# Earlier first evacuations, one tile loaded ahead of the weights, moved mask copies, and the last block projected by seven products, in a fused attention and SwiGLU kernel

## The chip, the cores and the metric

The kernel runs on one core of a Trainium2 chip. The time is device time of one execution in microseconds (us), the median of several runs. The profile is that of one execution; its span is some 1.7 to 2.1 us shorter than the time of the same run.

Engines: TensorE (PE) multiplies, VectorE (DVE) and ScalarE (ACT) read PSUM, compute and write SBUF, GpSimd (POOL) and SyncE (SP) mostly issue transfers here.

## The reference

Sliding-window attention with a distance bias, then a gated feed-forward layer:

```python
# q, k, v: (8, 8, 576, 64)   window 128
scores = np.where(mask, scale * (q @ k.T) + bias, -1e9)
attn = softmax(scores) @ v                   # (8, 8, 576, 64)
x = attn.transpose(0, 2, 1, 3).reshape(4608, 512)
g, val = x @ w_gate, x @ w_val               # (4608, 1536)
return (g * sigmoid(g) * val) @ w_out        # (4608, 512)
```

## The kernel before

Attention goes by units of 128 queries, 36 in all. The feed-forward layer goes by nine blocks of 512 tokens. For each block, 12 gate products (`pg`) and 12 value products (`pv`), each four matmuls of 512 columns, give the hidden rows `hT`. After a gate product ScalarE takes tanh (`tt`) and VectorE makes `uu` = (tanh + 1) times gate, and `hT` is `uu` times the value product. A projection (`po`) with `w_out` follows. Other names in the traces: `pt` are transposes of k and q (`kn`, `qn`), `ps` and `psc` scores, `ex` and `exc` their exponentials, `av` the product with v, `x` the attention output, `px` its transposes, `osb` output rows in SBUF on their way to a store.

In the traces here TensorE works through its instructions in the order in which they were built.

```python
        for i in range(FIRST):              # the first four units, a tile (128 tokens) each
            ...
            if i >= 2:
                begin(4, i - 1)             # gate and value products m=0, 1 over the tiles that exist
            if i > 0:
                x_transposed(i - 1)
        begin(6, 2)
        begin(4, 3)
        x_transposed(FIRST - 1)
        begin(6, 3)
        # cut: evacuation starts only with the full 512 columns, in gate_val

    load_qk(5, "k"); load_v(5)              # written on one line here
    load_w(1024, 1536)                      # last slices of w_gate and w_val, 512 KB each
    load(6)                                 # k, q, v of tile 6
```

Blocks 1 to 7 are projected by Strassen's scheme: the block as 2x2 quarters, seven products of 6 matmuls for each half in place of eight. The last block was not; it had 12 matmuls of 512 columns for each of three row groups and 24 of 256 for the fourth:

```python
        for j in range(3):
            for _ in project(NBLK - 1, j, ps_a, "a", 4):
                yield 1.0
        yield from last_project(NBLK - 1, 3)     # two halves of 256 columns, each stored by itself
```

The softmax here doesn't subtract the row's maximum and nothing guards it: scores larger than these inputs give would overflow.

## Time and profile before

| | before |
|---|---|
| time, median of 3 runs | 357.24 us (357.01 to 357.49) |
| span of the profiled run | 355.1 us |
| TensorE busy | 341.5 us (96%) |
| first scores of all (`ps`) start | 8.90 us |
| scores of unit 6 start | 44.81 us |
| first projection of block 0 (`po`) starts | 54.62 us |
| last block's projection, start to end | 340.65 to 351.20 us |
| behind it, to the end of the span | 3.9 us |

The prediction shows the lines on the ramp and the tail's products. The order of time on TensorE (start, duration, engine, line, operation, operands, shape, count) where the scores of unit 6 stand, and where the first projection of block 0 follows:

```profile
44.50 0.38 PE L368 MATMUL pg<-xT,wg_sb 128*128 128x512 f16 x1
44.81 0.62 PE L254 MATMUL ps<-qT,kT 64*128 64x256 f16 x8
...
54.62 1.24 PE L398 MATMUL po<-wo_sb,hT 128*128 128x512 f16 x5
```

The row to remember is the one at 44.81: exactly 9.81 us lie between it and the first `po`.

The DMA view of the last 17 us (345 to 362), in 40 slices of 0.425 us: busy tenths, GB/s, and issues with the number, the size and the median time to landing.

```profile
DMA  3994005895003997805800000000000000000000
GB/s 82 207 227 101 0 0 120 173 222 121 0 0 77 207 231 164 236 10 113 195 0 0 0 0 0 0 0 0 0 0 0 0 0 0 0 0 0 0 0 0
...
out_dram<-osb SPq DMA_DIRECT2D x5, 128.0 KB, 2.4
out_dram<-osb ACTq DMA_DIRECT2D x2, 64.0 KB, 2.2
out_dram<-osb SPq DMA_DIRECT2D x2, 64.0 KB, 2.1
```

The output leaves in bursts with pauses (the zeros) between them: each row group is stored while the next is projected. Only the last two half stores stand at the end.

### The profile page before, as it was taken

The numbers are of one execution on the slowest core, as the hardware profiler recorded it, in microseconds if no ns is written. First come the engines' busy times: TensorE is split into PE (matmuls) and PEld (weight loads), VectorE is DVE, ScalarE is ACT, GpSimd is POOL, SyncE is SP. The second block draws the span as 40 slices with busy tenths as digits, with TensorE's granted clock in tenths as the row PEclk, the third lists the DMA queues.
The fourth block names the chain that finished last, engine by engine and source line by source line (L and its number), as shares of the span: only waits on it lengthen the run. The fifth ranks groups of instructions, "written<-read, shape, count | busy, mean of one in ns | idle before, by whom it ended". The sixth has DMA issues, their size and how long they took to land.

```text
span 355.1 us, 7251 instructions
## 1 busy us (share of the span) xinstructions
PE 341.5 (96%) x2765; PEld 196.8 (55%) x2765; DVE 273.1 (77%) x595; ACT 178.2 (50%) x353; POOL 106.9 (30%) x132
## 2 busy tenths in 40 slices
PE   7898999999999999999999999999999999999995
PEld 4683454544456655565456655564666566456643
DVE  4858786997977799678986998799878965975540
ACT  4847584555555454555555555455444323332321
POOL 8964755544838354543500100000000000000000
PEclk9999999999999999999999999999999999999999
DMA  9999999999999999999995413311022101101114
GB/s 150 171 186 188 136 184 153 92 149 129 154 134 178 155 147 170 169 144 166 181 73 105 66 55 30 90 31 59 17 75 55 50 2 59 62 0 62 39 43 96
DMA packets 157763, 37.34 MB, mean 105 GB/s; under 512 B 147232, under 2 KB 153248, under 8 KB 157728
## 3 DMA queue, kind: packets, MB, share of 16 engines
q0 software_dynamic: 116224, 18.62, 84.3%
q1 hardware_dynamic: 41056, 17.97, 27.5%
q8 instruction: 21, 0.34, 0.4%
q10 hardware_dynamic: 448, 0.30, 0.3%
q14 instruction: 14, 0.11, 0.1%
HBM read 37.91 MB, written 9.44 MB: 133 GB/s over the span
## 4 chain that ended last, share of the span: by engine, by line
PE 71%; DVE 11%; DMA 6%; ACT 5%; POOL 4%; issue 3%; DVEq 0%; ACTq 0%; POOLq 0%
PE pg L368 21%; PE pv L368 21%; PE po L477 14%; PE av L319 4%; DMA qn<-in_q_dram 4%; PE po L398 3%; PE ps L254 3%; DVE uu L381 2%; DVE hT L385 2%; PE p L477 2%; DMA wv_sb<-in_moe_w_val_dram 2%; ACT ex L259 2%; PE px L345 2%; DVE ex L263 2%; ACT exc L286 1%
## 5 line engine op out<-in xcount | busy, mean ns | idle before, releaser
L368 PE MATMUL pg<-xT,wg_sb 128*128 128x512 f16 (+2 forms) x464 | 116.4, 365 | 0.3 <-ACT xT L346 0.2
L368 PE MATMUL pv<-xT,wv_sb 128*128 128x512 f16 (+2 forms) x464 | 114.7, 365 | 1.6 <-DVE uu L381 1.6
L379 ACT ACTIVATE tt<-pg 128x512 f16<-128x512 f32 x108 | 65.1, 604 | 85.7 <-PE pg L368 82.3
L381 DVE SCALAR_TENSOR_TENSOR uu<-tt,pg 128x512 f16<-128x512 f16 x107 | 73.0, 683 | 38.1 <-ACT tt L379 37.7
L385 DVE TENSOR_TENSOR hT<-uu,pv 128x512 f16<-128x512 f16 x108 | 73.7, 682 | 6.1 <-PE pv L368 2.3
L368 PEld LDWEIGHTS <-wv_sb 128*128 128x128 f16 x464 | 42.7, 98 | 38.8 <-issue 3.1
L368 PEld LDWEIGHTS <-wg_sb 128*128 128x128 f16 x464 | 42.4, 98 | 35.1 <-issue 2.9
L259 ACT ACTIVATE ex<-ps 128x512 f16<-128x512 f32 x96 | 50.1, 605 | 9.8 <-PE ps L254 9.8
L168 POOL DMA_DIRECT2D va<-in_v_dram x40 | 34.1, 856 | 50.3 <-PE av L319 36.0
L174 POOL DMA_DIRECT2D qn<-in_q_dram x39 | 33.6, 864 | 27.9 <-DMA qT<-qn 19.6
L174 POOL DMA_DIRECT2D kn<-in_k_dram x39 | 33.2, 860 | 25.6 <-DMA kT<-kn 15.7
L477 PEld LDWEIGHTS <-hT 128*128 128x128 f16 x336 | 31.8, 98 | 15.4 <-issue 3.5
L263 DVE TENSOR_TENSOR ex<-ex,m_reg 128x1024 f16<-128x1024 f16 x48 | 32.5, 686 | 8.3 <-ACT ex L259 8.3
L477 PEld LDWEIGHTS <-S 128*128 128x128 f16 x252 | 23.9, 98 | 11.7 <-issue 2.9
L322 DVE TENSOR_TENSOR x<-av,rec 128x256 f16<-128x256 f32 x72 | 28.9, 419 | 0.6
L477 PE MATMUL po<-T,S 128*128 128x256 f16 x168 | 23.0, 273 | 0.6 <-ACT p5s L495 0.6
L477 PE MATMUL po<-T,hT 128*128 128x256 f16 x168 | 23.1, 272 | 0.4
L286 ACT ACTIVATE exc<-psc 128x512 f16<-128x512 f32 x40 | 21.4, 608 | 3.4 <-PE psc L282 3.4
L346 ACT COPY xT<-px 128x512 f16<-128x512 f16 x24 | 14.1, 586 | 15.3 <-PE px L345 15.3
L319 PEld LDWEIGHTS <-ex 128*128 128x128 f16 x384 | 18.4, 97 | 4.9 <-issue 0.7
L319 PE MATMUL av<-va,ex 128*128 128x65 f16 x384 | 20.4, 193 | 0.5
L398 PE MATMUL po<-wo_sb,hT 128*128 128x512 f16 x84 | 19.7, 379 | 0.0
(74 smaller groups left out, 289.7 us busy)
## 6 DMA issues: line engine op xcount, KB each, us to landing
out_dram<-osb SPq DMA_DIRECT2D x32, 256.0 KB, 2.5
va<-in_v_dram POOLq DMA_DIRECT2D x32, 128.0 KB, 8.6
qn<-in_q_dram POOLq DMA_DIRECT2D x31, 128.0 KB, 8.7
kn<-in_k_dram POOLq DMA_DIRECT2D x31, 128.0 KB, 8.1
wo_sb<-in_moe_w_out_dram POOLq DMA_DIRECT2D x2, 768.0 KB, 9.4
wg_sb<-in_moe_w_gate_dram POOLq DMA_DIRECT2D x2, 512.0 KB, 10.7
wv_sb<-in_moe_w_val_dram POOLq DMA_DIRECT2D x2, 512.0 KB, 11.8
out_dram<-osb SPq DMA_DIRECT2D x6, 128.0 KB, 2.4
```

The source lines that it names most:

```text
L168: nc.gpsimd.dma_start(va[rank][p0:p1, :, 0:D], src)
L174: nc.gpsimd.dma_start(t_[p0:p1], src)
L259: nc.scalar.activation(e[:, o:o + 2, :], banks[q4][par], AF.Exp, scale=scale)
L263: nc.vector.tensor_mul(e[:, o, :], e[:, o, :], reg[:, o, :])
L319: nc.tensor.matmul(av[:, j, :], w, val, start=(n == 0), stop=(n == len(todo) - 1))
L322: nc.vector.tensor_mul(x[:, 4 * half:4 * half + 4, :], av[:, :, 0:D], rec.broadcast_to([P, 4, D]))
L368: nc.tensor.matmul(ps[:, c0:c1], w[:, kb, ms], xT[n][:, kb, c0:c1], start=(kb == 0 and c0 == 0), stop=(kb == NKB - 1 and c1 == 512))
L379: nc.scalar.activation(tt, pg, AF.Tanh, scale=0.5)
L381: nc.vector.scalar_tensor_tensor(out=uu, in0=tt, scalar=one if (n, m) == PIN else 1.0, in1=pg, op0=ALU.add, op1=ALU.mult)
L385: nc.vector.tensor_mul(hT[n][:, m, :], uu, pv)
L398: nc.tensor.matmul(po, hT[n][:, m, j * P:(j + 1) * P], wo_sb[:, m, :], start=(i == 0), stop=(i == NMB - 1))
L477: nc.tensor.matmul(dst, a[:, m, cols], b[:, m, :], start=(start and m == 0), stop=(m == HM - 1), skip_group_check=True)
```

## The change

It is meant to shorten both ends. On the ramp, the first two gate and value products are evacuated for the 384 tokens that exist, ahead of the last 128; k and q of tile 6 are loaded ahead of the last weight slices, as TensorE waits for that q; the mask copies leave the crowded stretch. At the end, the last block gets the seven products. The core of the diff:

```diff
+MASKS_AT = 18.0
@@ first_tiles
         begin(6, 2)
         begin(4, 3)
+        gate(0, 0, early[(0, 0, "g")][0], 0, 384)
         x_transposed(FIRST - 1)
+        val(0, 0, early[(0, 0, "v")][0], 0, 384)
+        gate(0, 1, early[(0, 1, "g")][0], 0, 384)
+        val(0, 1, early[(0, 1, "v")][0], 0, 384)
         begin(6, 3)
@@ loads
     load_qk(5, "k")
+    load_qk(6)
     load_v(5)
     load_w(1024, 1536)
-    load(6)
+    load_v(6)
@@ everything
-                if at == 5.0:
-                    make_masks()
         for step in steps:
+            if step == MASKS_AT:
+                make_masks()
@@ ffn, the last block
-        for j in range(3):
-            for _ in project(NBLK - 1, j, ps_a, "a", 4):
-                yield 1.0
-        yield from last_project(NBLK - 1, 3)
+        ends = [strassen(NBLK - 1, t) for t in range(2)]
+        for t in 7 * (0, 1):
+            next(ends[t])
+            yield 0.75
@@ strassen (end: the last block; t: its half)
+        if end and t:
+            store(n, t + 2, low, HC, DM, True)
...
-        nc.scalar.mul(low[:, 0:HC], X, 0.5)
-        (stores of top and low, all on SyncE)
+        store(n, t, top, 0, DM, end)             # end: the second of the two on ScalarE's queue
...
+        if end and t:
+            nc.vector.tensor_scalar_mul(low[:, 0:HC], X, 0.5)
+        else:
+            nc.scalar.mul(low[:, 0:HC], X, 0.5)
+        store(n, t + 2, low, 0, HC if end and t else DM, end)
```

Cut from it: the split of `gate_val` into `gate` and `val` over a range of columns, PSUM and SBUF buffers for the second half's copies, and the sums of `hT` for the last block.

More of the change, by code (lines that the diff above doesn't have):

```diff
@@ L368, in wide @@
             nc.tensor.matmul(ps[:, c0:c1], w[:, kb, ms], xT[n][:, kb, c0:c1],
-                             start=(kb == 0 and c0 == 0), stop=(kb == NKB - 1 and c1 == 512))
+                             start=(kb == 0 and c0 == 0), stop=(kb == NKB - 1 and c1 == 512),
+                             skip_group_check=(n == 0))
         if c1 < 512:
@@ L372, in wide, with gate, val, gate_val @@
         return ps
-    def gate_val(n, m):
+    acted = {}
+    def gate(n, m, pg, c0=0, c1=512):
+        if (n, m) not in acted:
+            acted[(n, m)] = [supool.tile([P, 512], FP16, name=i, tag=i) for i in ("tt", "uu")]
+        tt, uu = (t_[:, c0:c1] for t_ in acted[(n, m)])
+        nc.scalar.activation(tt, pg[:, c0:c1], AF.Tanh, scale=0.5)
+        nc.vector.scalar_tensor_tensor(out=uu, in0=tt, scalar=one if (n, m) == PIN else 1.0,
+                                       in1=pg[:, c0:c1], op0=ALU.add, op1=ALU.mult)
+    def val(n, m, pv, c0=0, c1=512):
         if n not in hT:
             hT[n] = hpool.tile([P, NMB, 512], FP16, name="hT", tag="hT")
-        pg = wide(n, m, "g")
-        tt = supool.tile([P, 512], FP16, name="tt", tag="tt")
-        nc.scalar.activation(tt, pg, AF.Tanh, scale=0.5)
-        uu = supool.tile([P, 512], FP16, name="uu", tag="uu")
-        nc.vector.scalar_tensor_tensor(out=uu, in0=tt, scalar=one if (n, m) == PIN else 1.0, in1=pg,
-                                       op0=ALU.add, op1=ALU.mult)
+        nc.vector.tensor_mul(hT[n][:, m, c0:c1], acted[(n, m)][1][:, c0:c1], pv[:, c0:c1])
+    def gate_val(n, m):
+        c0 = 384 if (n, m) in acted else 0
+        gate(n, m, wide(n, m, "g"), c0)
         yield
-        pv = wide(n, m, "v")
-        nc.vector.tensor_mul(hT[n][:, m, :], uu, pv)
+        val(n, m, wide(n, m, "v"), c0)
         yield
@@ L391, in rows_of, with store @@
         return [(0, 128, n * S + j * P)]
+    def store(n, j, osb, c0=0, c1=512, two=False):
+        for i, (p0, p1, r0) in enumerate(rows_of(n, j)):
+            (nc.scalar if two and i else nc.sync).dma_start(out[r0:r0 + p1 - p0, c0:c1],
+                                                            osb[p0:p1, c0:c1])
     def project(n, j, pool, tag, bufs):
@@ L402, in project @@
                 nc.scalar.mul(osb, po, 0.5)
-                for p0, p1, r0 in rows_of(n, j):
-                    nc.sync.dma_start(out[r0:r0 + p1 - p0, :], osb[p0:p1, :])
+                store(n, j, osb)
             yield
-    def last_project(n, j):
-        osb = opool.tile([P, DM], FP32, name="osb", tag="osb")
-        for half in range(2):
-            c = slice(half * DM // 2, (half + 1) * DM // 2)
-            po = ps_a.tile([P, DM // 2], FP32, name="po", tag="a", bufs=4)
-            for m in range(NMB):
-                nc.tensor.matmul(po, hT[n][:, m, j * P:(j + 1) * P], wo_sb[:, m, c],
-                                 start=(m == 0), stop=(m == NMB - 1))
-            if half == 0:
-                nc.scalar.mul(osb[:, c], po, 0.5)
-            else:
-                nc.vector.tensor_scalar_mul(osb[:, c], po, 0.5)
-            for i, (p0, p1, r0) in enumerate(rows_of(n, j)):
-                (nc.sync if i == 0 else nc.scalar).dma_start(out[r0:r0 + p1 - p0, c], osb[p0:p1, c])
-            yield 1.5
     HM = NMB // 2
@@ L467, in strassen @@
         cols = slice(t * P, (t + 1) * P)
-        po = ps_f.tile([P, 2, HC], FP32, name="po", tag="po", bufs=1)
+        end = n == NBLK - 1
+        pool, tag, bufs = (ps_a, "a", 4) if end and t else (ps_f, "po", 1)
+        po = pool.tile([P, 2, HC], FP32, name="po", tag=tag, bufs=bufs)
         p2 = ps_a.tile([P, HC], FP32, name="p2", tag="a")
         top, low = (opool.tile([P, DM], FP32, name="osb", tag="osb") for _ in range(2))
-        p1s = supool.tile([P, HC], FP32, name="p1s", tag="p1s", bufs=1)
-        p5s = supool.tile([P, HC], FP32, name="p5s", tag="p5s", bufs=1)
-        u2s = supool.tile([P, HC], FP32, name="u2s", tag="u2s", bufs=1)
+        if end and t:
+            spare = [opool.tile([P, DM], FP32, name="osb", tag="osb") for _ in range(2)]
+            p1s, p5s, u2s = spare[0][:, 0:HC], spare[0][:, HC:DM], spare[1][:, 0:HC]
+        else:
+            p1s, p5s, u2s = (supool.tile([P, HC], FP32, name=i, tag=i, bufs=1)
+                             for i in ("p1s", "p5s", "u2s"))
         def product(dst, a, b, start=False):
@@ L501, in strassen @@
         half_plus(top[:, HC:DM], Y, u2s)
+        store(n, t, top, 0, DM, end)
         yield
         product(X, A22, T4)
-        nc.scalar.mul(low[:, 0:HC], X, 0.5)
-        for j, osb in ((t, top), (t + 2, low)):
-            for p0, p1, r0 in rows_of(n, j):
-                nc.sync.dma_start(out[r0:r0 + p1 - p0, :], osb[p0:p1, :])
+        if end and t:
+            nc.vector.tensor_scalar_mul(low[:, 0:HC], X, 0.5)
+        else:
+            nc.scalar.mul(low[:, 0:HC], X, 0.5)
+        store(n, t + 2, low, 0, HC if end and t else DM, end)
         yield
@@ L534, in ffn @@
                         weight_sums(m // 2 - 1)
-                if 0 < n < NBLK - 1 and m >= 9:
+                if n > 0 and m >= 9:
                     sums(n, m - 9)
```

## The prediction

> **What bounds the kernel now.** I read the page of the profile first, then the table of busy time by stretch, then the order of time around the gaps that the table shows, then the DMA view.
>
> ```profile
> span 355.1 us, 7251 instructions
> PE 341.5 (96%) x2765; PEld 196.8 (55%) x2765; DVE 273.1 (77%) x595; ACT 178.2 (50%) x353; POOL 106.9 (30%) x132
> ...
> 20.00:30.00 10.00, 8.41 (x112) 6.59 (x109) 5.75 (x13) 6.24 (x13) 5.86 (x7) 1.00 1.72 186
> 30.00:40.00 10.00, 9.01 (x57) 3.99 (x56) 7.29 (x12) 5.43 (x11) 5.66 (x9) 1.00 1.94 176
> 200.00:250.00 50.00, 49.76 (x387) 28.27 (x386) 44.83 (x101) 25.44 (x51) 0.88 (x1) 1.00 0.22 53
> 350.00:356.00 6.00, 1.20 (x11) 0.82 (x9) 0.42 (x1) 0.31 (x1) 0.00 (x0) 0.83 0.39 87
> ```
>
> In the table the first number after the stretch is its length, the next is TensorE's busy time. TensorE (PE) is the bound: it idles 13.6 of 355.1 us, at a full clock. From 40 to 350 us it idles only about 3.4 us, so a change there must take products away; time won earlier is kept. The rest of the idle time is the ramp (1.6 us in 20 to 30, 1.0 in 30 to 40, 3.7 before 20) and the tail, 3.9 us after the last product. The change aims at both ends.
>
> ```profile
> 25.21 0.69 DVE L381 SCALAR_TENSOR_TENSOR uu<-tt,pg 128x512 f16<-128x512 f16 x1 [4.07 <-ACT tt L379]
> 28.14 0.68 DVE L381 SCALAR_TENSOR_TENSOR uu<-tt,pg 128x512 f16<-128x512 f16 x1
> 28.87 1.04 PE L368 MATMUL pv<-xT,wv_sb 128*128 128x512 f16 x4 [1.15 <-DVE uu L381]
> 37.34 0.40 PE L201 MATMUL pt<-idm,qn 128*128 128x128 f16 x4 [0.81 <-DMA qn<-in_q_dram]
> ...
> 24.32 12.98 DMA qn<-in_q_dram
> ```
>
> These give start, duration, engine, and in brackets the idle time before and what ended it. The reader is to see that VectorE (DVE) sat idle 4.07 us, began the first evacuation at 25.21, and was then late: its third `uu`, which frees a PSUM buffer, ends at 28.82, and TensorE, out of buffers, waits 1.15 us for it. A second gap, 0.81 us, is q of tile 6: issued at 24.32 behind the two last W slices, landed 12.98 us later.
>
> ```profile
> 4.61 2.56 ACT L92 ACTIVATE m_reg<-stage 128x256 f16<-128x256 f32 x8 [1.68 <-DMA stage<-distance]
> 9.32 4.21 ACT L259 ACTIVATE ex<-ps 128x512 f16<-128x512 f32 x8 [2.14 <-PE ps L254]
> 26.23 0.63 ACT L109 COPY m_c<-m_reg 128x512 f16<-128x512 f16 x1
> 28.53 0.60 ACT L379 ACTIVATE tt<-pg 128x512 f16<-128x512 f32 x1
> ...
> 340.65 7.93 PE L398 MATMUL po<-wo_sb,hT 128*128 128x512 f16 x36
> 348.42 2.78 PE L414 MATMUL po<-wo_sb,hT 128*128 128x256 f16 x24
> 351.24 0.42 DVE L419 TENSOR_SCALAR osb<-po 128x256 f32<-128x256 f32 x1 [9.08 <-PE po L414]
> ```
>
> The four mask copies hold ScalarE (ACT) from 26.23 to 28.53, 2.30 us, among the first tanh; ScalarE has an idle hole of 2.14 us before 9.32. The last block's projection takes TensorE from 340.65 to 351.20, 10.55 us, with nothing else left to do.
>
> **What the Trainium skill says.** "TensorE: Matmul & The Clock Gate", section "Back-to-back issue gap": a warm matmul of N columns costs N/2.4 + 2.5 ns, so 216 ns for 512 and 109 for 256; for streams with weight loads it also names 131 ns for 512. The trace agrees with the first and not with the second: the chain of waits gives 7.77 us to the 36, 216 ns each, and 2.63 us to the 24, 109.6. "PSUM — Partial Sum Buffer", section "Terms": TensorE writing a bank while VectorE or ScalarE reads it is a collision error. That bears on evacuating 384 columns while the last 128 of the same bank are still to be written: the two must take turns. No wait of this kind is in the trace of before; in the built order of the changed kernel it is there (below). "DMA: Bandwidth & Descriptors", section "Issuing engines are not separate DMA queues": all queues share the same 16 engines, so moving a load ahead delays others. The trace agrees in kind: loads here land 8 to 13 us after issue while the DMA row of the page shows 9s.
>
> **The change part by part.** I worked from the built instruction order with what each wait is for.
>
> First evacuations. New on ScalarE and VectorE: tanh, `uu`, `hT` for 384 columns of m=0 and m=1, then the rest of 128. From 0.69 us for 512 columns and 0.42 for 256, VectorE's 384 take about 0.55 and 128 about 0.28; tanh (0.60 and 0.38) 0.49 and 0.27. Gate 0's third tile is written at 22.20 and done at 22.59; tanh 22.6 to 23.1, `uu` to 23.7, `hT` to 24.35. The next xT copy stays at 23.52 to 24.11 on ScalarE, so the second tanh follows it, to 24.52; `uu` to 25.10, `hT` to 25.76. In the built order each product of the last 128 columns waits for the VectorE read of its own bank: gate 0 for 23.7 and value 0 for 24.35, harmless; gate 1 for 25.10 (before: 24.60) and value 1 for 25.76. So TensorE gets two new gaps, 0.51 and 0.44 us, and the m=3 gate starts near 26.47, not 25.50. Then the gain: the 128-column pieces are done by 26.94, tanh of m=2 ends 27.04 (no mask copies), its `uu` 27.76, and the m=3 value product starts at 27.80 instead of 28.87. Seven of the twelve transposes that stood before it now stand behind it, 0.40 us, so the net is 0.67. Small gaps up to 32.3 (0.23 us) close as well: 0.9 us gained in all.
>
> Tile 6 ahead of the W slices. k and q of tile 6 are issued near 20 and 21 us rather than 23.44 and 24.32, and land near 31 (10 us as its neighbours take). Needed near 36: the 0.81 us gap goes. The last value slice, landed at about 35.4, lands some 2 us later (256 KB ahead of it at 170 to 190 GB/s is 1.4 us, plus later issue), 37.3; its first reader is at about 39. Not a wait, with 1.8 us to spare.
>
> Masks. Meant to come later, but that call now lies outside the manually ordered region, and the built order has the four copies directly behind the eight mask exponentials, ahead of the first `ex`. They run from about 7.2 to 9.5, into the hole of 2.14 us that ends at 9.32: the first `ex` slips by 0.15 to 0.2 us, and since ScalarE is busy without a break until 13.5, I charge 0.15.
>
> Last block. Before: 36 products of 512 columns and 24 of 256. After: 14 groups of 6 of 256, 84 x 109 ns = 9.16 against 7.77 + 2.63 = 10.40 us: 1.24 less. The 12 sums (0.42 us each, 5.0 us of VectorE) lie beside the last gate and value products: VectorE is idle about 1 to 1.7 us before each of the last tanh results. By my walk through the built order the last `hT` ends at 342.3 and the last S2 at 343.4; TensorE wants `hT` at 342.5 and S2 at 343.7. No wait, but with 0.2 to 0.3 us to spare. The tail behind the last product is the same (0.42 us on VectorE, two half stores); but five stores now go out on each of two queues within 3 us, 0.50 to 0.54 us an issue, and on ScalarE a store stands ahead of its last scaling. I charge 0.25. Net 1.0.
>
> Sum: 0.9 + 0.8 + 0.1 (part of a 0.18 us wait at 35.3) - 0.15 + 1.0 = 2.65 us; 357.24 - 2.65 = 354.6 us.
>
> **The rivals.** First: the bank waits cost what the early evacuation gains. For it: they are in the built order, and the second tanh stands behind the xT copy, which makes them real. Against: VectorE's four-microsecond hole is used, and the buffer wait they replace is 1.15 us. If TensorE gains nothing here: 355.5. Second: the transfers move the wait. `wo` lands at 52.5 to 52.7 and its last rows are read first, at 54.62; 1.7 us earlier is 52.9. If its loads slip behind the W slices, the ramp's gain is given back there: 355.5 to 356. Against: the same bytes stand ahead of it, and the queue looks full. Third: the tail is latency and VectorE, not products: S sums late by 1 us and stores queueing would leave 0.2 of the 1.2: 355.4. Against: a pair of stores near 336 us moved at 235 GB/s with the DMA engines 63% busy, so about 370 GB/s is there (an estimate), and the last three microseconds need at most 340. Two rivals together: 356.3. On the good side, if the bank waits are shorter than worked out and tail and loads are free: 353.5.
>
> **Range and chances.** 354.6, with 353.3 to 356.0 for 8 in 10: a gain of 1.2 to 3.9 us. 2% is 7.1 us, more than the ramp gaps and the saved products together; a loss of 7 us would need the rivals and a new stall in the steady stretch, where the instruction order is the same. Faster 0.02, same 0.97, slower 0.01.
>
> **What would show it.** On TensorE in 24 to 26 us, two waits of about half a microsecond on `uu` and `hT`; the m=3 value product near 27.8; no wait for q of tile 6; mask copies at 7 to 9.5 us. After 345 us, 84 products of 256 columns in about 9.2 us without a wait on S2, and a tail of about 4 us behind them. Wrong if TensorE idles for W slices near 38 us, for `wo` near 53, or if the order of the last sums holds the products up.

## More of the kernel before

While the attention units run, products of the current block are placed between them: TensorE does a few `pg` and `pv` matmuls while ScalarE and VectorE work on a unit's scores.

Up to the first projection of block 0, all filling comes from block 0.

## The result, and the profile after

| | before | after |
|---|---|---|
| time, median | 357.24 us | 356.34 us (356.10 to 356.55, 4 runs) |
| span of the profiled run | 355.1 | 354.7 |
| first scores of all | 8.90 | 9.16 |
| scores of unit 6 | 44.81 | 44.07 |
| first `po` of block 0 | 54.62 | 53.88 |
| last block's projection | 340.65 to 351.20 | 340.03 to 349.50 |
| behind it | 3.9 | 5.2 |

The ratio of the times is 0.9974, with a 95% interval of 0.9957 to 0.9992. Here and below a ratio is the mean time of one kernel's fast runs over that of the other's in the same rounds, so it is not quite the quotient of the medians quoted beside it. The change gains 0.9 us, where 2.65 were predicted; 356.34 lies above the predicted range, which ended at 356.0. The class (within 2%) was right.

The span splits without a rest: up to the first `po` it is 0.74 us shorter; from there to the last product 0.96 shorter (296.58 to 295.62); behind it 1.3 longer. Sum -0.40, and 355.1 became 354.7. That is less than the 0.9 us of the medians because the two profiled runs are not typical: the one of before took 356.89 us, below all three that were timed, and the one of after took 356.55, the slowest of its four. Its first scores also start 0.26 us later (9.16 against 8.90), which differs from run to run (see the second group); counted from the first scores, the first `po` comes 1.00 us earlier.

First the head of the page and the table of busy time by stretch (stretch, its length, then TensorE's busy time), for after:

```profile
span 354.7 us, 7335 instructions
...
20.00:30.00 10.00, 9.12 (x117) 7.14 (x114) 6.54 (x17) 4.92 (x12) 5.82 (x8) 1.00 1.82 181
30.00:40.00 10.00, 9.72 (x73) 4.87 (x71) 8.49 (x16) 7.05 (x14) 5.85 (x9) 1.00 1.81 182
50.00:60.00 10.00, 9.27 (x80) 4.62 (x78) 6.81 (x16) 6.07 (x13) 5.25 (x6) 1.00 2.26 160
```

TensorE's idle time falls from 1.59 to 0.88 us in 20 to 30 and from 0.99 to 0.28 in 30 to 40: 1.42 us are won by 40. Then the third row: before, TensorE was busy for 9.80 us of 50 to 60; now 9.27. The same row of before:

```profile
50.00:60.00 10.00, 9.80 (x95) 5.09 (x95) 6.36 (x16) 6.59 (x13) 5.25 (x6) 1.00 2.24 160
```

Another 0.12 us go in 40 to 50 (9.84 to 9.72). Almost half of what was won early is idled away later.

The order of time on TensorE shows the early part much as predicted, bank waits included (in brackets the idle time before the row and what ended it):

```profile
25.40 0.38 PE L369 MATMUL pg<-xT,wg_sb 128*128 128x128 f16 x4 [0.33 <-DVE uu L384]
26.06 0.38 PE L369 MATMUL pv<-xT,wv_sb 128*128 128x128 f16 x4 [0.28 <-DVE hT L391]
...
28.07 1.02 PE L369 MATMUL pv<-xT,wv_sb 128*128 128x512 f16 x4
...
35.89 0.39 PE L202 MATMUL pt<-idm,qn 128*128 128x128 f16 x4
...
43.32 0.81 PE L369 MATMUL pg<-xT,wg_sb 128*128 128x512 f16 x3
44.07 0.61 PE L255 MATMUL ps<-qT,kT 64*128 64x256 f16 x8
...
51.38 0.29 PE L346 MATMUL px<-idm,x 128*128 128x128 f16 x2 [0.23 <-DVE x L323]
...
53.88 1.89 PE L415 MATMUL po<-wo_sb,hT 128*128 128x512 f16 x8
```

The two bank waits are there (0.33 and 0.28 us), the m=3 value product starts at 28.07 rather than 28.87, and q of tile 6 is transposed at 35.89 without a wait, 1.45 us earlier than the 37.34 of before. But the scores of unit 6 come only 0.74 us earlier than before. The last thing before them is three gate matmuls; before, it was one. Then come waits for VectorE's `x` at 51 and 52 us which the kernel before did not have, and the first `po` stands 9.81 us behind the scores, to the hundredth as before.

The tail, in order of time: the last product on TensorE, the store issues on ScalarE's queue (ACTq, with how long the engine was held and how many), ScalarE's last scaling, VectorE's last scaling.

```profile
347.33 2.14 ACTq L407 DMA_DIRECT2D out_dram<-osb  x3
...
348.03 1.47 PE L481 MATMUL po<-T,hT 128*128 128x256 f16 x12
...
349.54 0.42 DVE L512 TENSOR_SCALAR osb<-po 128x256 f32<-128x256 f32 x1 [0.91 <-PE po L481]
...
349.57 0.38 ACT L514 ACTIVATE osb<-po 128x256 f32<-128x256 f32 x1 [3.71 <-PE po L481]
349.98 1.38 ACTq L407 DMA_DIRECT2D out_dram<-osb  x2
```

The first row: ScalarE issues three stores from 347.33 to 349.47 (0.58, 0.78 and 0.58 us, with short pauses). Its scaling of the first half, whose product ended about 0.65 us before the last one (at about 348.85), starts only behind them, at 349.57. Its two last issues, the first half's store and behind it the second half's, then run to 351.36, 1.86 us after the last product; SyncE has two there as well. Before, VectorE's last scaling ended at 351.66 and only half stores were left.

And the DMA view of the same 17 us for after:

```profile
DMA  0000100068999878962000000000000000000000
GB/s 0 0 0 0 39 0 0 0 137 205 207 304 371 299 183 188 350 191 53 0 0 0 0 0 0 0 0 0 0 0 0 0 0 0 0 0 0 0 0 0
...
out_dram<-osb ACTq DMA_DIRECT2D x3, 128.0 KB, 3.0
...
out_dram<-osb ACTq DMA_DIRECT2D x2, 64.0 KB, 2.6
```

The bursts with pauses have become one block of eleven slices, 4.7 us: the two halves take turns product by product, so all the output becomes ready near the end. The half stores on ScalarE's queue land after 2.6 us, those of before on the same queue after 2.2.

### The profile page after: what moved, and what is told of

Same layout as the page of the kernel before. It is cut to its first block, busy times and chain, and to the rows that moved or that the text cites. A ratio compares the mean times of both kernels' runs of the same rounds, so it can differ in the third digit from the quotient of the medians.

```text
span 354.7 us, 7335 instructions
## 1 busy us (share of the span) xinstructions
PE 340.5 (96%) x2789; PEld 200.0 (56%) x2789; DVE 279.8 (79%) x617; ACT 179.4 (51%) x358; POOL 106.9 (30%) x132
## 4 chain that ended last, share of the span: by engine, by line
PE 73%; DVE 16%; ACT 7%; issue 3%; DVEq 0%; ACTq 0%
PE pv L369 21%; PE pg L369 20%; PE po L481 16%; PE av L320 4%; DVE uu L384 3%; DVE hT L391 3%; PE ps L255 3%; PE p L481 3%; DVE ex L264 3%; ACT ex L260 2%; PE px L346 2%; ACT exc L287 2%; ACT tt L383 1%; DVE x L323 1%; PE pt L202 1%
## 5 line engine op out<-in xcount | busy, mean ns | idle before, releaser
L383 ACT ACTIVATE tt<-pg 128x512 f16<-128x512 f32 (+2 forms) x110 | 65.5, 596 | 85.0 <-PE pg L369 81.5
L384 DVE SCALAR_TENSOR_TENSOR uu<-tt,pg 128x512 f16<-128x512 f16 (+2 forms) x109 | 73.4, 674 | 32.0 <-ACT tt L383 31.3
L391 DVE TENSOR_TENSOR hT<-uu,pv 128x512 f16<-128x512 f16 (+2 forms) x110 | 74.0, 673 | 7.0 <-PE pv L369 2.2
L481 PEld LDWEIGHTS <-hT 128*128 128x128 f16 x384 | 36.4, 98 | 16.3 <-issue 3.5
L481 PEld LDWEIGHTS <-S 128*128 128x128 f16 x288 | 27.4, 98 | 12.3 <-issue 2.9
L481 PE MATMUL po<-T,S 128*128 128x256 f16 x192 | 26.0, 273 | 0.6 <-ACT p5s L499 0.6
L481 PE MATMUL po<-T,hT 128*128 128x256 f16 x192 | 26.1, 272 | 0.5
L255 PE MATMUL ps<-qT,kT 64*128 64x256 f16 x192 | 17.2, 272 | 1.0 <-DVE qT L207 0.8
```

What stands on the lines that cost most here:

```text
L383: nc.scalar.activation(tt, pg[:, c0:c1], AF.Tanh, scale=0.5)
L384: nc.vector.scalar_tensor_tensor(out=uu, in0=tt, scalar=one if (n, m) == PIN else 1.0, in1=pg[:, c0:c1], op0=ALU.add, op1=ALU.mult)
L391: nc.vector.tensor_mul(hT[n][:, m, c0:c1], acted[(n, m)][1][:, c0:c1], pv[:, c0:c1])
L481: nc.tensor.matmul(dst, a[:, m, cols], b[:, m, :], start=(start and m == 0), stop=(m == HM - 1), skip_group_check=True)
```

## The experiments

Each ran five rounds (one gave four values) beside the kernel before, on one chip per group (banks_pool came later than the rest of its group, on another chip). All gave the right result unless said otherwise. The kernel before measured 357.05 to 357.28 us as the median of the group. Where two kernels of different groups are compared, the ratios are the safer guide, as each is taken against the kernel before on its own chip.

### First group: tail or ramp, and two ways to mend the tail

**tail_only** is the kernel before with only the last block's part of the change. **ramp_only** is the opposite: the changed kernel with the old last block.

```diff
 # ramp_only, from the changed kernel (tail_only is the mirror image, from before)
-        ends = [strassen(NBLK - 1, t) for t in range(2)]
-        for t in 7 * (0, 1): ...
+        for j in range(3): ... project(NBLK - 1, j, ps_a, "a", 4)
+        yield from last_project(NBLK - 1, 3)
```

> The kernel before with nothing changed but the last block's projection. Theory A (the shorter products are won, 1.1 to 1.2 us, and lost again behind them, because the last two stores are issued 0.6 us later after the last product and land 0.5 to 0.7 us slower): the time stays at 357.0 to 357.4 us, ratio 0.999 to 1.001. Theory B (the prediction's term: a net gain of 1.0 us at the end): 356.2 to 356.4 us, ratio 0.997 to 0.998.

> The changed kernel with the old projection of the last block. Theory A (the ramp gains 1.4 us by 40 us and keeps 0.7 to 0.8 of it, as TensorE then runs out of products between 50 and 54 us): 356.4 to 356.6 us, ratio 0.9975 to 0.998. Theory B (the 1.65 us of the prediction are kept and the profiled run is only a late one): 355.6 us, ratio 0.9955.

Measured: tail_only 357.33 us (ratio 1.0006, 0.9994 to 1.0019), ramp_only 356.71 us (0.9985, 0.9971 to 0.9998). The tail by itself gains nothing. In tail_only's trace the stretch from the first `po` to the last product is 295.47 us, against 296.58 before: the products do save 1.1 us. The part behind the last product takes 5.1 us instead of 3.9, and takes it all back. ramp_only keeps the 3.9.

**vec_scale** lets VectorE do the first half's last scaling, which stood behind ScalarE's store issues.

```diff
-        if end and t:
+        if end:
             nc.vector.tensor_scalar_mul(low[:, 0:HC], X, 0.5)
```

> The changed kernel with the last scaling of the first half moved from ScalarE to VectorE, so that it no longer stands behind ScalarE's store issues. Theory A1 (the issue order sets the end): the last two stores are issued about 0.6 us earlier, at 0.45 us after the last product, and the time falls by 0.5 us against the changed kernel, to 355.7 to 355.9 us. Theory A2 (the amount stored in the last three microseconds sets the end): the stores go out earlier and land slower, and the time stays within 0.2 us of the changed kernel's 356.3.

Measured: 356.00 us (0.9971, 0.9958 to 0.9983), between its two theories: 0.3 us below the changed kernel by the medians, 0.1 by the ratios, and the two intervals overlap. The scaling now runs at 348.83 us in VectorE's row, and still there are 5.2 us behind the last product in the profiled run, its slowest. A late scaling is a small part of the tail at most.

**stagger** lets the first half run ahead, so that it is stored earlier, on SyncE's queue alone.

```diff
-        for t in 7 * (0, 1):
+        for t in (0, 1, 0, 1) + 5 * (0,) + 5 * (1,):
...
-        store(n, t, top, 0, DM, end)
+        store(n, t, top, 0, DM, end and t)
```

> The changed kernel with the two halves of the last block in turn for their first two products and then one half wholly ahead of the other, the first half stored from SyncE's queue alone. No more than 384 KB then goes out in the last 2.5 us, and no store issue stands ahead of ScalarE's copies. Theory A (order and traffic of the stores cost 1.1 to 1.3 us): the tail behind the last product falls from 5.2 to about 4.0 us and the time to 355.0 to 355.4 us, if the products in one half do not wait for the reads of their bank. Theory B (the longer tail is chance, or of the products themselves): 356.1 to 356.5 us. If products wait for reads of their own bank, TensorE idles between 343 and 350 us and up to 1 us of it is lost again.

Measured: 357.87 us (1.0020, 1.0007 to 1.0032), slower than before. The tail did shrink, to 3.9 us. But two products of a half that share a PSUM bank now follow each other closely, and TensorE waits for the bank to be read: 1.7 us in four waits of 0.31 to 0.57, as the profile counts them. The last product ends at 352.19 instead of 349.50. So this mend failed, and its tail says little for the theory: products that come later may also leave the stores more time. banks below has the same order without the waits, and a tail of 4.8 us.

### Second group: the ramp's parts

**load_only**, **gate_only** and **mask_only** are the kernel before with one part of the ramp's change each, by the diff above. Without the early evacuation, TensorE's built order is that of before.

> The kernel before with only k and q of tile 6 loaded ahead of the last W slices; gates, masks and the last projection as before, so TensorE's order is the same. The 0.81 us wait for q of tile 6 near 37 us should go. Theory 1 (what is won at 37 us is kept, because the scores of unit 6 come earlier by it): about 0.7 us faster, 356.4. Theory 2 (the chain from the scores of unit 6 to the first product of the projection has a fixed length and TensorE runs out of block 0's products before its end, so a win that does not move the scores is given back by 54 us): the scores themselves waited for this q here, so they move by up to 0.7 and theory 2 gives the same 356.4; only if the value slice or wo now comes late is it 357.0.

> The kernel before with only the first evacuations for 384 tokens; loads, masks and last projection as before. The mask copies now stand between the first tanh and the later ones on ScalarE. Theory 1 (early evacuation is a gain that lasts): 0.4 to 0.6 us faster, 356.7. Theory 2 (the two waits for VectorE's reads of the same bank eat it, and the q of tile 6, which still lands near 37.3, holds the scores of unit 6 where they were): 0.0 to 0.2 us faster, 357.0 to 357.2; the wait for that q then grows above 0.81 us by whatever was won before it.

> The kernel before with only the mask copies moved, from 26.2 us to directly behind the mask exponentials near 7 us. Theory 1: VectorE's third uu comes sooner as ScalarE is free at 26 us, worth 0.1 to 0.4 us on TensorE there, then lost at the wait for q of tile 6, which grows by the same: 357.0 to 357.2, the same. Theory 2 (the copies delay the first ex by 0.15 us and this goes through to the end): 357.2 to 357.4.

| | time | ratio (95%) | unit 6 scores minus first scores | unit 6 scores to first `po` |
|---|---|---|---|---|
| before | 357.24 | | 35.91 | 9.81 |
| mask_only | 357.32 | 1.0002 (0.9990 to 1.0015) | 36.17 | 9.82 |
| gate_only | 358.73 | 1.0047 (1.0034 to 1.0060) | 36.94 | 9.60 |
| load_only | 356.35 | 0.9969 (0.9956 to 0.9981) | 34.91 | 9.82 |
| ramp_only | 356.71 | 0.9985 (0.9971 to 0.9998) | 35.10 | 9.82 |
| changed kernel | 356.34 | 0.9974 (0.9957 to 0.9992) | 34.91 | 9.81 |

The fourth column is taken from the first scores of all because these start between 8.74 and 9.36 us from run to run, whatever the kernel. Kernels with one and the same ramp differ in it by up to 0.2 us. The last column is not like the others for gate_only: 16 `av` matmuls that elsewhere stand ahead of the first `po` stand behind it there.

load_only came in at the time that both its theories gave (356.4): loading k and q of tile 6 earlier is worth 1.1 us by itself (0.9 by the medians), all that the whole ramp gains. The masks are worth nothing. That the early evacuation by itself costs time was expected by neither theory: 1.7 us by the ratio, 1.45 by the medians, as one of the five runs took 359.89. gate_only's rows on TensorE say why:

```profile
37.59 0.40 PE L202 MATMUL pt<-idm,qn 128*128 128x128 f16 x4 [1.46 <-DMA qn<-in_q_dram]
...
45.96 0.61 PE L255 MATMUL ps<-qT,kT 64*128 64x256 f16 x8
...
53.95 0.28 PE L346 MATMUL px<-idm,x 128*128 128x128 f16 x2 [0.66 <-DVE x L323]
```

What the evacuation wins at 26 us goes into the wait for q of tile 6, which lands when it lands: 1.46 us instead of 0.81. Then the scores of unit 6 come at 45.96, more than 1 us later than before. Counted in the rows from that transpose to the scores, 28 gate and value matmuls stand between the two, where before there were 25: three more, of 0.216 us each, are 0.65 us; 0.25 is the later transpose (37.59 against 37.34), and 0.1 a wait at 43.44. With the scores late, block 0's products run out and TensorE waits for `x` near 54 us, 0.66 and 0.32 us. By the twelfth matmul of the first projection (58.82 against 57.32) all of the loss is there: 1.5 us, and the two spans differ by 1.6.

In the changed kernel 27 stand there, two more than before. So the early evacuation shifts the order in which the scheduler fills in products: more of them in front of the scores, fewer left behind.

**pace3** tries to turn this around on the changed kernel, with attention three steps ahead throughout block 0.

```diff
-                target = base + max(0, step - ALONE) + ...
+                target = base + 3 + max(0, step - ALONE) + ...
```

> The changed kernel with attention paced three steps ahead in the first block, so that fewer products stand before the scores of unit 6 and more of them are left to fill the time of its latency chain (the only other edit: none). Theory 1 (TensorE runs out of block 0's products between 50 and 54 us because too many stand before the scores): the waits of 0.23 and 0.32 us there shrink, the first product of the projection comes 0.3 to 0.5 us earlier, and the time is 355.9 to 356.1. Theory 2 (the stretch from scores to projection is set by the engines' rate there, not by where the filler stands): same as the changed kernel, 356.3 to 356.5, or slower if scores now wait for tiles that have not landed.

Measured: 361.96 us (1.0126, 1.0111 to 1.0142). The scores came earlier, at 42.81, but so did attention work that follows them: the transposes of the next tiles now stood in front of the projection, and TensorE waited 3.4 us for their q and k, whose loads are issued behind 1.5 MB of `w_out`. The first `po` slid to 58.53. The edit was too blunt to test what it was meant to test.

### Third group: bytes at the end, and finer mends

**half_unstored** gives a wrong result: it leaves the four stores of the last block's first half out of the tail, and writes zeros there before that block begins.

```diff
+            if n == NBLK - 1:     # zeros for the first half's rows, in two column halves
+                nc.sync.dma_start(out[...], zero[...])
...
-        store(n, t, top, 0, DM, end)
+        if t or not end:
+            store(n, t, top, 0, DM, end)     # and the store of low likewise
```

> The changed kernel with a wrong result on purpose: the four stores of the last block's first half (0.5 MB) are taken out of the tail; zeros go to those rows before the last block begins. All products and sums stay, so both queues have no more than three stores to issue at the end and 0.5 MB less is in flight. Theory 1 (the 1.3 us lost behind the last product are late issues and a crowded end of the transfers): the tail behind the last product shrinks from 5.2 to about 4.0 us, 355.1 to 355.4. Theory 2 (the tail is the latency of the last scaling and the last store alone): no change, 356.2 to 356.5.

Measured: 355.62 us (0.9959, 0.9946 to 0.9971). Behind the last product there are 3.6 us, less than before's 3.9 and less than the 4.0 expected. The time missed its mark by 0.3 us because the ramp was disturbed: this run's first `po` was at 54.82, 0.94 later than the changed kernel's, with a new wait of 0.4 us for the value slice. The memset of the zeros on GpSimd ahead of the loads is the likely reason, not shown.

**three_queues** is vec_scale with the first half's second stores on GpSimd's queue.

```diff
-            (nc.scalar if two and i else nc.sync).dma_start(...)
+            (nc.gpsimd if two and i and j % 2 == 0
+             else nc.scalar if two and i else nc.sync).dma_start(...)
```

> As vec_scale (the first half's last scaling on VectorE), and the first half's second stores are issued by GpSimd, idle by then, not by ScalarE. If issuing is what holds the last stores back: the last issue comes 0.3 to 0.6 us earlier than in vec_scale, 355.5 to 355.8. If the transfers are what is late: the same as vec_scale, 355.9 to 356.2. GpSimd's issues may themselves be slower, then 356.5.

Measured: 356.71 us (0.9984, 0.9971 to 0.9996), no better than vec_scale and probably worse; 5.6 us behind the last product, and landings of 3.1 us on GpSimd's queue.

**load_tail** is load_only with the last block by seven products and vec_scale's mend.

> The kernel before with only k and q of tile 6 ahead and the last block by seven products with vec_scale's mend: no early evacuation, masks where they were. If the two gains found alone (1.1 us of load_only, 0.3 us of vec_scale against the changed kernel, with the tail alone at 0.0) add up: 355.7 to 355.9, faster than the changed kernel. If the early evacuation is worth something beside the load: 356.2 or more.

Measured: 356.17 us (0.9972, 0.9959 to 0.9984). It is not as fast as the sum expected, because the seven products still give back most of what they win (4.8 us behind the last one). The expectation gave 356.2 or more if the evacuation is worth something, and 356.17 is close to that mark. But vec_scale, which differs from it only in having the early evacuation and the moved masks, has the same ratio (0.9971), so the two together are worth nothing there that these runs can tell. The rows on TensorE agree:

```profile
36.60 0.39 PE L202 MATMUL pt<-idm,qn 128*128 128x128 f16 x4
...
44.07 0.62 PE L255 MATMUL ps<-qT,kT 64*128 64x256 f16 x8
...
53.88 1.89 PE L415 MATMUL po<-wo_sb,hT 128*128 128x512 f16 x8
```

Compare the changed kernel: q transposed at 35.89, 0.71 us earlier, thanks to the evacuation. But the scores of unit 6 start at 44.07 in both, and the first `po` at 53.88 in both. (Their first scores start within 0.03 us of each other.) The 0.71 us are gone 8 us later: 0.43 of them are the two matmuls more in front of the scores, and 0.11 a wait at 41.89.

**pace_early** is vec_scale with attention three steps ahead only while the step is below 15.

```diff
+                target = base + (3 if step < 15 else 0) + max(0, step - ALONE) + ...
```

> As vec_scale, with attention paced three steps ahead, but only while step is below 15 (pace3 kept it up through the whole first block, which put the transposes of tile 9 ahead of its loads). Built order: 142 gate and value products stand before the scores of unit 6, not 147, and the transposes of tile 9 stay where they were. Theory 1 (the first product of the projection follows the scores of unit 6 by some 9.7 us, whatever was won before them): the scores come near 43.0, the waits on x in 50 to 54 us shrink, and the time is 355.4 to 355.6, 0.4 to 0.6 better than vec_scale. Theory 2 (the stretch is bound by the rate of the engines there): 355.9 to 356.2.

Measured: 355.78 us (0.9962, 0.9948 to 0.9975). The interval overlaps that of vec_scale, so the gain in time is a lead, and the trace carries the point:

```profile
42.62 0.62 PE L255 MATMUL ps<-qT,kT 64*128 64x256 f16 x8
...
53.33 0.60 PE L415 MATMUL po<-wo_sb,hT 128*128 128x512 f16 x2 [0.52 <-DVE hT L391]
```

The scores come 1.43 us before vec_scale's 44.05, the first `po` 0.54 before its 53.87; 0.27 of both is the earlier start of this run (first scores at 8.74 against 9.01), so 1.16 and 0.27 are the edit's. The waits on `x` are gone. The distance is now 10.71 us and no longer 9.81, as the first `po` waits 0.52 us for VectorE's last `hT` of block 0. So the 9.81 us are no fixed distance: with the scores early enough, another wait comes last, here that for VectorE.

### Fourth group: what of the tail is issues and what is bytes

**no_store** leaves the first half's stores out with nothing in their place (those rows stay unwritten). **few_bytes** keeps the four issues but stores 32 columns in each. Both are wrong.

```diff
 # few_bytes
-        store(n, t, top, 0, DM, end)
+        store(n, t, top, 0, DM if t or not end else 32, end)     # and low likewise
```

> The changed kernel with the first half's four stores of the last block simply left out (result wrong on purpose, those rows stay unwritten). Unlike half_unstored nothing is added at the start, so the ramp is the changed kernel's. The tail behind the last product should be the 3.6 us that half_unstored had, against 5.2: 354.7 to 354.9. If it is 355.6 again, half_unstored's ramp was not what cost it time, and the tail is not worth 1.5 us.

> The changed kernel with the first half's four stores kept as eight-fold to sixteen-fold narrower ones, 32 columns each (result wrong on purpose): as many issues on both queues as before, but 0.47 MB less to move. If issues hold the tail back (1.3 us late by five issues of half a microsecond on each queue): like the changed kernel, 356.0 to 356.4. If bytes do: like no_store, 354.7 to 355.1. If both share it: about 355.5.

Measured: no_store 354.81 us (0.9932, 0.9919 to 0.9944), few_bytes 355.76 us (0.9959, 0.9946 to 0.9971). These two intervals are apart. Their last issues on ScalarE's queue, no_store's first, then that of few_bytes:

```profile
349.80 0.50 ACTq L407 DMA_DIRECT2D out_dram<-osb  x1
```

```profile
349.72 1.37 ACTq L407 DMA_DIRECT2D out_dram<-osb  x2
```

No_store's last issue is done at 350.30, 1.0 us after its last product (349.30), and 2.7 us later the span ends. Few_bytes has two issues there, done at 351.09, 1.54 us after its last product; 2.9 us remain. In the changed kernel it was 1.86 and 3.3. The split of the 1.5 us that the first half's stores cost is less clean than planned, because few_bytes did not keep all its issues where they were. 32 columns of the first store are ready early, and its two issues left the crowd:

```profile
342.95 0.58 ACTq L407 DMA_DIRECT2D out_dram<-osb  x1
```

SyncE's stands at 342.94. So 0.95 us are there with two more issues near the end, one on each queue, and hardly any bytes (355.76 - 354.81; of this 0.7 lie behind the last product in the traces, 4.4 us against 3.7). The other 0.58 (356.34 - 355.76) come with the bytes and with the two issues that had moved; here the intervals overlap. The traces of no_store and the changed kernel split the tail without few_bytes: the last issue is done 0.86 us later after the last product (1.86 against 1.0), and what is behind it is 0.6 longer (3.3 against 2.7). That is nearest to the third branch of the expectation, both share it, with later issues the larger part. What of the 0.6 is bytes is not shown.

**banks** is pace_early with stagger's order, but X, Y and p2 of each half in PSUM banks of their own. **banks_load** is the same last block on load_tail.

```diff
+        if end:
+            X = ps_a.tile([P, HC], FP32, name="po", tag="a")
+            Y = ps_a.tile([P, HC], FP32, name="po", tag="a")
+            p2 = ps_f.tile([P, HC], FP32, name="p2", tag="gv", bufs=3)
...
+        for t in (0, 1, 0, 1) + 5 * (0,) + 5 * (1,):
```

> pace_early with the last block's two halves no longer in turn: the first half runs ahead and is stored, on SyncE's queue alone, while the second half's last five products run; and X, Y and p2 of each half lie in PSUM banks of their own, which stagger's did not. If stagger lost its time to reads of a bank that TensorE wanted next (1.7 us there), those waits shrink to 0.3 us or less in all, the last product ends within 0.3 us of pace_early's 348.7, and behind it are 3.6 to 4.2 us, not 5.2: 354.5 to 355.0. If the crowd of transfers at the end was not the cause: 355.8 or more.

> The same last block on load_tail (only k and q of tile 6 ahead, no early evacuation, no new pacing). The ramp there cost 0.4 us more than pace_early's: 354.9 to 355.4. Told apart with it: whether the early evacuation and the pacing are still worth anything once the tail is mended.

Measured: banks 355.42 us (0.9947, 0.9933 to 0.9961), banks_load 355.93 us (0.9958, 0.9946 to 0.9971). With own banks the order costs TensorE nothing: 295.34 us from first `po` to last product, where load_tail has 295.53, and no waits. The tail is 4.8 and 4.9 us, and both times lie above the ranges expected. For banks the tail is 0.4 less than pace_early's, but load_tail, with the old order, already had 4.8, so these traces do not show that the order shortens the tail. (Among the correct kernels whose halves take turns, all stores on two queues, it is 4.8 to 5.2 us; with the old projection it is always 3.9.) It stayed above the 4.2 expected: SyncE had seven stores to issue, and the last began at 349.92, 1.1 us after the last product.

**banks_pool** moves the first half's last store, two of those issues, to GpSimd.

> As banks, but the first half's last store (two issues) goes out on GpSimd's queue, so that SyncE is free when the second half's outputs are ready. In banks SyncE's last issue began 1.1 us after the last product and the tail was 4.8 us. If late issues are what is left of the tail: the last issue begins about 0.5 us after the last product, the tail is 4.0 to 4.3 us and the time 354.8 to 355.1, against 355.42. If the crowd of bytes holds the rest: 355.3 to 355.6.

Measured: 355.21 us (0.9953, 0.9939 to 0.9967), not separable from banks. SyncE's last issue now begins at 349.43, 0.63 us after the last product, about as expected, and ScalarE's at 349.47. The tail is 4.5 us, not 4.0: ScalarE's last issue holds 0.77 us, and its 128 KB store lands after 3.1 us. That the bytes under way, 1 MB close to the end, are the reason is likely and not shown.

banks and banks_pool are the fastest correct kernels found, about 1 us faster than the changed kernel and 2 us faster than before, by medians. Between banks and the changed kernel the intervals touch by 0.0004.

## Why the prediction was wrong

The landmarks of four traces, in us:

| | first `po` | first `po` to last product | behind it | span |
|---|---|---|---|---|
| before | 54.62 | 296.6 | 3.9 | 355.1 |
| changed kernel | 53.88 | 295.6 | 5.2 | 354.7 |
| load_only | 53.49 | 296.6 | 3.9 | 354.0 |
| no_store (wrong result) | 53.71 | 295.6 | 3.7 | 353.0 |

By the prediction's steps:

- **Early evacuation, +0.9 us: failed.** The rows came as worked out, with the m=3 value product at 28.07 (predicted 27.80, in a run that started 0.26 us later), and 0.7 us were there at 36 us. The step that failed is the sentence behind the sum: "so a change there must take products away; time won earlier is kept." It is not kept: of the 0.7 us nothing is left at the first `po`. load_tail has no early evacuation and its scores of unit 6 and first `po` are at the same hundredth. The evacuation changed the built order: 27 matmuls instead of 25 between q of tile 6 and the scores of unit 6, and with the scores no earlier, TensorE ran out of block 0's products behind them and waited 0.23 and 0.32 us for `x`. Alone, without the earlier load, the evacuation costs 1.5 to 1.7 us. I had read the built order for the waits but not for what stands in front of what after 32 us.
- **Tile 6 ahead, +0.8 us and 0.1 for a small wait: right.** 1.1 us alone, 1.0 by the scores of unit 6. It is the whole ramp gain, because that q released the scores that everything behind waits for.
- **Masks, -0.15 us: right in place, wrong in size.** The four copies ran from 6.96 to 9.24 us, about as predicted (7.2 to 9.5). The first `ex` after them waited for TensorE anyhow; mask_only shows no difference.
- **The second rival (weight slices and `w_out` late): did not happen** in the changed kernel; no wait for either. It came in pace3 in another form, with tiles behind `w_out`.
- **Seven products, 1.24 us less: right.** 10.55 became 9.47 us, 1.08 less, without a wait on S2, one of the sums of hidden rows that the products read.
- **"The tail behind the last product is the same" and the charge of 0.25 us for issues: failed.** The tail grew from 3.9 to 5.2 us. The term is the 0.25, measured at 1.3. no_store shows that the first half's four stores cost 1.5 us there: the last issue is done 0.86 us later after the last product, and what follows it takes 0.6 longer. The prediction saw the five stores on each queue and charged 0.25 for them; two of them on each queue are issued after the last product, the first half's last store ahead of the second's. The third rival in the prediction (stores queueing) was the right one; I argued it away with a bandwidth figure, which tells nothing of the time it takes to issue and to land.

Together: predicted 1.65 on the ramp plus 1.0 at the end. Measured 0.74 at the first `po` (1.00 counted from the first scores), and from there on 0.96 minus 1.3. In the prediction's own sum, evacuation 0.9 becomes 0, tile 6 with the small wait 0.9 becomes 1.0, masks -0.15 become 0, the products' 1.24 become 1.08 and the charge of 0.25 becomes 1.3: 0.8 us, near the 0.9 measured. The prediction's figure for two rivals together, 356.3, is what came, but by luck: its first rival, that the bank waits eat the gain, did not happen. They cost 0.61 us as the trace counts them, and 0.7 us were still won behind them. Both mistakes are of one kind: a gain was followed to the place where it arises and not to the end.

What stays open: why the scheduler puts more products in front of the scores when their evacuation is early (the counts are shown, the reason was not looked for); whether beside the earlier load the evacuation is worth zero or costs up to 0.5 us, as ramp_only against load_only would have it with overlapping intervals; and how much of the tail is bytes and how that comes about.

## What to carry to other kernels

Follow a gain on a busy engine to the next place where that engine runs out of filling. Here the position of the work that starts a latency chain decided, not how early the filling was done, and an edit shifted the built order so that more filling stood in front of that work. At the end of a program, count stores and their issues per queue behind the last product, not only products: the sequence that made all outputs ready together paid here with queued issues and slower landings. Take one part of a change alone on the chip before believing a sum; here one load was the whole gain; the early evacuation alone lost, and the seven products alone gained nothing.

## What the Trainium skill lacked or had wrong

- "DMA: Bandwidth & Descriptors", section "Issuing engines are not separate DMA queues", says that issuing on several engines only saves sequencer time, "which is usually small relative to the DMA itself." For stores of 64 to 128 KB it was not small: 0.47 to 0.78 us to issue against 2.0 to 3.5 us to landing, and at the end of the program four stores more put off the end of the last issue by 0.86 us after the last product (changed kernel against no_store).
- The same page, section "Anatomy of one DMA — SWDGE (gpsimd) path", fits 2.0 us plus bytes/436e3, for GpSimd's queue. By that fit (an estimate from the page) 128 KB take 2.3 us. GpSimd's two stores of 128 KB took 3.1 us in three_queues and 2.6 in banks_pool, with other stores in flight; the fit has no term for a crowded end.
- "TensorE: Matmul & The Clock Gate", section "Back-to-back issue gap", names 131 ns sustained for 512 columns with weight loads and calls the isolated formula too long there. Here the formula held: 216 ns for 512 columns (7.77 us for 36, before), and 109 ns for 256 (1.31 us for 12 in the chain that ended last, changed kernel) against its 109.
- "PSUM — Partial Sum Buffer", section "Terms", tells that two engines must not meet in a bank, not what taking turns costs: waits of 0.33 and 0.28 us in the changed kernel and 0.31 to 0.57 us in stagger, and none in the last block with a bank for each accumulator (banks).
